# Attention, mixing, weight rounding and the first MLP tile placed by a plan in time

## The chip, the cores and the metric

The kernel runs on one core of a Trainium2 chip. The core has five engines that run side by side: TensorE (PE in the profile, its weight loads PEld), VectorE (DVE), ScalarE (ACT), GpSimd (POOL) and SyncE (SP, which here only issues DMAs). Each engine takes its instructions strictly in the order in which the program lists them for it; semaphores make it wait for other engines or for DMAs. The metric is the device time of one execution in microseconds (us); lower is better.

## The reference

Two parts follow each other. The first is causal attention with a decaying bias over 8 batches, 8 heads, 576 positions and head size 64:

```python
scores = scale * np.matmul(q, k.transpose(0, 1, 3, 2))
cum = np.cumsum(np.maximum(s, 0.0), axis=-1)
bias = -(cum[:, :, :, None] - cum[:, :, None, :])
scores = np.where(causal, -1000000000.0, scores + np.minimum(bias, 0.0))
attn = softmax(scores)          # with + 1e-09 in the denominator
x = np.matmul(attn, v)          # then [8, 576, 512]
```

The second mixes by a two-dimensional Fourier transform, normalises, and runs an MLP of width 2048:

```python
mixed = np.real(np.fft.fft(np.fft.fft(x, axis=1), axis=2))
u = x + mixed
un = (u - mean(u)) / np.sqrt(var(u) + 1e-06)
out = u + np.maximum(un @ w_ch1, 0.0) @ w_ch2
```

All of it is single precision. The kernel keeps that precision on TensorE by splitting numbers into a high and a low part ("h" and "l" in the names) and adding three products, high by high, high by low and low by high. The MLP weights arrive as 64-bit floating-point words and are rounded to 32 bits on the chip.

## The kernel before

**Attention.** Work goes by pairs of heads, `i` from 0 to 31, four pairs to a batch. For each pair `load` fetches q and k, `high` (L613, L615, ACT) and `low` (L630 DVE, L633 POOL, with two DMAs that move rows between partitions) split them, `maxes` (L654 PE, L661 DVE) computes the rows' maxima from high-part scores, and a small transpose and DMA (L666 to L669) put them into the operand as one more row. `scores` (L686, L687 PE) then computes transposed scores with the maximum already taken off, ACT takes the exponential into `P` (L690), and POOL zeroes the upper triangle (L693, L696). `av` (L718) multiplies by V, `recip` (L733 to L739) inverts the row sums and spreads them over partitions by a round trip through memory, and `finish` (L754 to L758) scales. While pair `i` has its scores taken, pair `i-1` is in `av`, pair `i+1` in `maxes` and `low`, pair `i+2` in `high`.

**Mixing.** Once a batch's four pairs are finished, `folds` (L448 to L464) adds and subtracts mirrored positions and `fourier` (L481 to L538) does the two transforms as matrix products, adds them to x and stores the sum in `uD`.

**Weights.** There are 16 chunks `f`, each in four pieces of 256 columns. `rounded` (L78 to L89) loads one piece and rounds it with four DVE instructions, one on ACT and one on POOL. `convert_w` does so for the first `NC = 6` chunks during attention, with one buffer, and stores the result in `wD`; `load_w` fetches those again, rounds the other ten itself, splits each into high and low (L115 ACT, L117 DVE or POOL) and keeps the second layer's part in `w2D`. The chunks live in three pools that take over memory as attention (`N0 = 3` chunks, then up to `N1 = 8`) and the last mixing give theirs back.

**MLP.** Tokens go in nine tiles of 512. `ln_tile` normalises a tile, `plain` or `block` splits it. `first_tile` (L339 first product, L343 and L344 rectifier and split, L262 to L264 second product) runs chunk after chunk as weights become ready. The other eight tiles run in `fast_tile` (L378), a seven-product scheme that needs sums of weights (`sums_w`, L143 to L163) and of token blocks (`combine`).

**What sets the order.** In attention and the first tile the order comes from `weave`: each function is a generator that yields a cost of its own scale, and of several such streams the one least advanced in proportion to its total goes next. Only PE keeps that order exactly (`tc.manual_schedule(engines={PE})`); on the other engines the framework's own scheduler may reorder. From the second tile on all engines keep the written order (`tc.manual_schedule()`). The line that decides this for attention:

```python
order.enter_context(tc.manual_schedule(engines={mybir.EngineType.PE}))
```

Of the kernel before, what the change touches and what calls it, by code (L numbers as in the profile page):

```python
# [27 lines left out]
NC = 6  # L28
NC1 = 4.5
N0 = 3  # L30
# [4 lines left out]
CH = [(128, 0, 576, 0), (128, 128, 448, 128), (128, 256, 320, 256), (128, 320, 256, 384), (64, 320, 256, 512)]  # L35
# [5 lines left out]
def fused_kernel(ctx, tc, qkT, vA, sP, wP, tabD, tabS, corr, out):  # L41
# [31 lines left out]

    def rounded(pool, f, x, bufs):

        m = pool.tile([128, WC], I32, tag="wm", name="wm", bufs=bufs)
        raw = pool.tile([128, 2 * WC], I32, tag="raw", name="raw", bufs=bufs)
        nc.sync.dma_start(out=raw, in_=wP[f, :, WC * x:WC * x + WC].bitcast(I32))  # L78
        hi = raw.rearrange("p (n w) -> p n w", w=2)[:, :, 1]
        lo = raw.bitcast(U16).rearrange("p (n w) -> p n w", w=4)[:, :, 1]  # L80
        yield 0.0
        e = pool.tile([128, WC], I32, tag="we", name="we", bufs=bufs)
        nc.vector.tensor_scalar(e, hi, 0x7FF00000, None, op0=ALU.bitwise_and)  # L83
        nc.scalar.activation(e, e, AF.Relu, bias=wbias, scale=8.0)
        nc.vector.tensor_scalar(m, hi, 0xFFFFF, 0x100000, op0=ALU.bitwise_and, op1=ALU.bitwise_or)  # L85
        yield 0.4
        nc.vector.scalar_tensor_tensor(out=e, in0=hi, scalar=-0x80000000, in1=e, op0=ALU.bitwise_and, op1=ALU.bitwise_or)  # L87
        nc.vector.scalar_tensor_tensor(out=m.bitcast(F32), in0=lo, scalar=2.0 ** -16, in1=m, op0=ALU.mult, op1=ALU.add)  # L88
        nc.gpsimd.tensor_mul(e.bitcast(F32), m.bitcast(F32), e.bitcast(F32))  # L89
        yield 0.4  # L90
        return e.bitcast(F32)

    def convert_w(pool, lo, hi, bufs):

        for f in range(lo, hi):
            for x in range(1024 // WC):
                m = yield from rounded(pool, f, x, bufs)
                nc.sync.dma_start(out=wD[f, :, WC * x:WC * x + WC], in_=m)
                yield 0.2

    def load_w(pool, f):

        wh = pool.tile([128, 512], F32R, tag=f"wh{f}", name=f"wh{f}")
        wl = pool.tile([128, 512], F32R, tag=f"wl{f}", name=f"wl{f}")
        vh, vl = second()
        W[f], W2[f] = (wh, wl), (vh, vl)
        if f < NC:
            nc.sync.dma_start(out=wl.bitcast(F32), in_=wD[f, :, 0:512])
            nc.sync.dma_start(out=vl.bitcast(F32), in_=wD[f, :, 512:1024])
        n = 512 if f < NC else WC  # L110
        for x in range(1024 // n):
            h, low = (wh, wl) if x * n < 512 else (vh, vl)
            xs = slice(n * x % 512, n * x % 512 + n)
            m = low[:, xs].bitcast(F32) if f < NC else (yield from rounded(stage, f, x, nstage))
            nc.scalar.copy(h[:, xs], m)  # L115
            yield 0.2 * n / 512
            last_subs[x * n >= 512] = (nc.vector if x * n < 512 else nc.gpsimd).tensor_sub(low[:, xs], m, h[:, xs].bitcast(F32))  # L117
            yield 0.2 * n / 512
        nc.sync.dma_start(out=w2D[0, f], in_=vh.bitcast(F32))
        nc.sync.dma_start(out=w2D[1, f], in_=vl.bitcast(F32))  # L120

    last_subs = [None, None]
# [202 lines left out]
    def first_tile(t0):  # L325
        _, r = LN[t0]
        acc = accs()
        fetch, done = writer(t0, acc, r)
        bl = BL.pop(t0)
        for f in range(NF):  # L330
            while min(f + 2, NF) not in W and next(feed, None) is not None:
                pass
            wh, wl = W[f]
            h = bank("h")
            for k in range(2):
                i = 0
                for a, b in ((wh, 0), (wl, 0), (wh, 1)):
                    for j in range(4):
                        nc.tensor.matmul(h[:, 256 * k:256 * k + 256], a[:, j * 128:(j + 1) * 128], bl[j // 2, k][b][:, j % 2], start=i == 0, stop=i == 11)  # L339
                        i += 1  # L340
            zh = zp.tile([128, TOK], F32R, tag="zh", name="zh", bufs=3)
            zl = zp.tile([128, TOK], F32R, tag="zl", name="zl", bufs=3)
            nc.scalar.activation(zh, h, AF.Relu)  # L343
            nc.vector.scalar_tensor_tensor(out=zl, in0=h, scalar=0.0, in1=zh.bitcast(F32), op0=ALU.max, op1=ALU.subtract)  # L344
            for g in groups():
                g()
            held.append((acc, zh, zl, f, done))
            yield 1.0
        for _ in range(3):
            fetch()  # L350

# [67 lines left out]
    cor = fft.tile([33, 258], F32R, name="cor")  # L419
    eh = fft.tile([33, 289], F32R, name="eh")  # L420
    nc.vector.memset(eh.bitcast(F32), 0.0)
# [5 lines left out]
    nc.vector.memset(Aw[:, 576:577], 0.0)  # L427

    def load_tables():
        for i in range(2):  # L430
            nc.gpsimd.dma_start(out=dcos[i], in_=tabD[i, :, :, 0:258])
            nc.gpsimd.dma_start(out=dsin[i], in_=tabD[i, :, :, 258:514])
            nc.gpsimd.dma_start(out=scos[i], in_=tabS[i, 0:97, 0])
            nc.gpsimd.dma_start(out=ssin[i], in_=tabS[i, 0:96, 1])
# [4 lines left out]
    FOURIER = 8900  # L439

    def folds(b, xa, xs):
# [3 lines left out]
        e = fft.tile([1, 289], F32, tag="e", name="e")  # L445
        for jj in range(2):
            a = Aw
            nc.vector.tensor_add(a[:, 0:576], xa[:, jj], xs[:, jj])  # L448
            bb = fft.tile([128, 576], F32, tag="Bw", name="Bw")
            nc.gpsimd.tensor_sub(bb, xa[:, jj], xs[:, jj])  # L450
            yield 1.0
            d = fft.tile([128, 289], F32, tag="Df", name="Df")
            nc.vector.tensor_add(d, a[:, 0:289], a[:, 576:287:-1])
            split(De[0][:, jj], De[1][:, jj], d)
            yield 1.0
            d = fft.tile([128, 289], F32, tag="Df", name="Df")
            nc.vector.tensor_sub(d[:, 0:288], bb[:, 1:289], bb[:, 575:287:-1])
            split(Do[0][:, jj], Do[1][:, jj], d[:, 0:288])
            yield 1.0
# [5 lines left out]
        folded[b] = (De, Do)  # L465

    folded = {}
    FOLDS = 7
    MIX = ((0.3, 0.25), (0.3, 0.4), (1, 0.35), (1, 0.05))

    def fourier(b, xa, xs):
# [402 lines left out]
    for _ in feed:  # L874
        pass
# [178 lines left out]
```

## Time and profile before

| | |
|---|---|
| median of 3 runs | 1455.16 us (1451.71 to 1459.55) |
| the profiled execution | 1451.0 us, span 1449.3 us, mean TensorE clock 0.959 |
| busy, share of the span | PE 1307.2 us (90%), DVE 891.4 (62%), ACT 640.7 (44%), POOL 513.7 (35%) |
| attention, to the last product with V | from 0 to 565 us |
| rest of mixing, first tile, second tile | 565 to 842 us |
| tiles 3 to 9 | 842 us to the end |

The shares over the span are a mean over stages that differ, so a table of stretches is the view to begin with. A clock below 1 in a stretch is the share of full speed that TensorE was granted there. A wait is put down to the instruction that came last among those it waited for. A busy PE is not always PE at its peak, since the ends of its matmuls are modelled.

### The profile page before, as it was taken

The numbers are of one execution on the slowest core, as the hardware profiler recorded it, in microseconds if no ns is written. First come the engines' busy times: TensorE is split into PE (matmuls) and PEld (weight loads), VectorE is DVE, ScalarE is ACT, GpSimd is POOL, SyncE is SP. The second block draws the span as 40 slices with busy tenths as digits, with TensorE's granted clock in tenths as the row PEclk, the third lists the DMA queues.
The fourth block names the chain that finished last, engine by engine and source line by source line (L and its number), as shares of the span: only waits on it lengthen the run. The fifth ranks groups of instructions, "written<-read, shape, count | busy, mean of one in ns | idle before, by whom it ended". The sixth has DMA issues, their size and how long they took to land.

```text
span 1449.3 us, 21855 instructions
## 1 busy us (share of the span) xinstructions
PE 1307.2 (90%) x7534; PEld 1111.8 (77%) x7534; DVE 891.4 (62%) x2018; ACT 640.7 (44%) x1507; POOL 513.7 (35%) x526
## 2 busy tenths in 40 slices
PE   4898979898989897697759999999999999999998
PEld 3675867676867675686548888888888888888887
DVE  6667687778677777577987754445445444554423
ACT  4675756566656656243433333333333333323321
POOL 6345465655546566464465211110211102021100
PEclk9998989999989998799979999999999999999999
DMA  8565556556555555534543353443435244342433
GB/s 205 138 175 143 155 143 180 144 161 177 149 156 141 168 130 184 181 103 164 162 136 118 103 187 102 145 133 127 164 102 180 98 145 146 124 167 88 146 116 116
DMA packets 125657, 210.18 MB, mean 145 GB/s; under 512 B 16488, under 2 KB 41417, under 8 KB 125547
## 3 DMA queue, kind: packets, MB, share of 16 engines
q1 hardware_dynamic: 123099, 204.79, 46.7%
q0 software_dynamic: 1632, 2.43, 0.8%
q10 hardware_dynamic: 816, 1.57, 0.3%
q8 instruction: 59, 0.97, 0.3%
q14 instruction: 51, 0.42, 0.1%
HBM read 153.33 MB, written 31.46 MB: 127 GB/s over the span
## 4 chain that ended last, share of the span: by engine, by line
PE 45%; DVE 8%; POOL 4%; DMA 2%; issue 1%; ACT 1%; SPq 0%; POOLq 0%; DVEq 0%; ACTq 0%
PE b L378 21%; PE acc L263 8%; PE acc L264 8%; PE acc L262 8%; POOL we L89 1%; DVE we L87 1%; DVE wm L85 1%; DVE we L83 1%; DVE bl L231 1%; POOL w2l L117 1%; DVE wm L88 1%; POOL t L210 0%; DMA rd<-sums 0%; DVE wl L117 0%; DMA rb<-rd 0%
## 5 line engine op out<-in xcount | busy, mean ns | idle before, releaser
L264 PE MATMUL acc<-zl,w2h 128*128 128x512 f32 x576 | 230.2, 401 | 11.1 <-DVE zl L344 11.1
L262 PE MATMUL acc<-zh,w2h 128*128 128x512 f32 x576 | 230.7, 401 | 7.2 <-ACT zh L343 7.2
L263 PE MATMUL acc<-zh,w2l 128*128 128x512 f32 x576 | 229.8, 399 | 0.0
L718 PE MATMUL pavB<-P,va 128*128 128x320 f32 (+2 forms) x640 | 198.3, 399 | 7.7 <-ACT stage L722 7.1
L690 ACT ACTIVATE P<-ps 128x320 f32<-128x320 f32 (+4 forms) x384 | 145.0, 390 | 112.1 <-PE ps L687 107.3
L654 PE MATMUL pm<-KQ 128*128 128x256 f32 (+4 forms) x384 | 157.0, 427 | 35.6 <-DVE Mx L661 18.7
L309 POOL TENSOR_TENSOR w<-w,o 128x512 f32<-128x512 f32 x32 | 43.7, 1375 | 382.5 <-DVE o L305 339.7
L686 PE MATMUL ps<-KQ 128*128 128x256 f32 (+3 forms) x384 | 153.1, 401 | 23.7 <-ACT P L690 12.9
L661 DVE CUSTOM_DVE_ANT_0 trash<-pm,amask 128x128 bf16<-128x128 f32 (+3 forms) x256 | 123.7, 483 | 74.1 <-PE pm L654 57.1
L370 ACT ACTIVATE zh<-cs 128x256 fp32r<-128x256 f32 (+1 forms) x128 | 67.2, 525 | 163.6 <-DVE cs L390 101.2
L264 PEld LDWEIGHTS acc<-zl,w2h 128*128 128x128 f32 x576 | 109.9, 191 | 37.8 <-DVE zl L344 12.4
L718 PEld LDWEIGHTS pavB<-P,va 128*128 128x128 f32 (+1 forms) x640 | 105.0, 194 | 30.9 <-issue 12.6
L371 DVE SCALAR_TENSOR_TENSOR zl<-cs,zh 128x256 fp32r<-128x256 f32 (+1 forms) x128 | 75.7, 592 | 79.3 <-ACT zh L370 79.3
L262 PEld LDWEIGHTS acc<-zh,w2h 128*128 128x128 f32 x576 | 110.1, 191 | 14.6 <-ACT zh L343 9.0
L687 PE MATMUL ps<-q,k 128*128 128x256 f32 (+3 forms) x384 | 120.2, 316 | 0.6 <-POOL q L633 0.6
L378 PEld LDWEIGHTS b<-bh,wh 128*128 128x128 f32 x512 | 96.3, 189 | 28.4 <-DVE cs L390 6.2
L654 PEld LDWEIGHTS pm<-KQ 128*128 128x128 f32 (+1 forms) x384 | 70.4, 186 | 61.6 <-DVE Mx L661 27.2
L633 POOL TENSOR_TENSOR q<-qk,q 64x576 fp32r<-64x576 f32 x64 | 99.9, 1575 | 42.7 <-DMA q<-KQ 36.4
L263 PEld LDWEIGHTS acc<-zh,w2l 128*128 128x128 f32 x576 | 110.2, 191 | 5.0
L686 PEld LDWEIGHTS ps<-KQ 128*128 128x128 f32 (+1 forms) x384 | 72.6, 189 | 49.8 <-ACT P L690 19.1
L378 PE MATMUL b<-bh,wh 128*128 128x256 f32 x512 | 102.9, 282 | 4.9 <-DVE cs L390 4.9
L378 PE MATMUL b<-bh,wl 128*128 128x256 f32 x512 | 103.4, 284 | 0.0
(173 smaller groups left out, 2859.7 us busy)
## 6 DMA issues: line engine op xcount, KB each, us to landing
w2h<-w2D SPq DMA_DIRECT2D x128, 256.0 KB
w2l<-w2D SPq DMA_DIRECT2D x128, 256.0 KB
qk<-in_qkT_dram SPq DMA_DIRECT2D x32, 576.0 KB
raw<-in_wP_dram SPq DMA_DIRECT2D x64, 256.0 KB
va<-in_vA_dram SPq DMA_DIRECT2D x32, 480.0 KB
q<-KQ SPq DMA_DIRECT2D x32, 288.0 KB
k<-KQ SPq DMA_DIRECT2D x32, 288.0 KB
rb<-rd SPq DMA_DIRECT2D x64, 144.0 KB
```

What stands on the lines that cost most here:

```text
L262: nc.tensor.matmul(acc[j], a[:, cs], y, start=f == 0, stop=False)
L263: nc.tensor.matmul(acc[j], b[:, cs], y, start=False, stop=False)
L264: nc.tensor.matmul(acc[j], a[:, cs], z, start=False, stop=f == NF - 1)
L371: nc.vector.scalar_tensor_tensor(out=y[1][:, at], in0=src, scalar=0.0, in1=y[0][:, at].bitcast(F32), op0=ALU.max, op1=ALU.subtract)
L378: nc.tensor.matmul(p[:, 0:256], a[:, j * 128:(j + 1) * 128], b[:, j], start=start and i == 0, stop=i == 5, skip_group_check=not start)
L633: nc.gpsimd.tensor_sub(q1[64:128, h], qk[0:64, h], q1[0:64, h].bitcast(F32))
L654: nc.tensor.matmul(p[:nq, :n], qy[:, h, 128 * c:128 * c + nq], ky[:, h, k0:k0 + n], start=True, stop=True)
L661: nc.vector.tensor_tensor_reduce(out=trash[:nq, :n], in0=p[:nq, :n], in1=amask[:nq, m0:m0 + n], scale=1.0, scalar=first if x else NEG, op0 ...
L686: nc.tensor.matmul(p[:nk, :n], ky[:, h, ksl], qy[:, h, a:a + n], start=True, stop=False)
L687: nc.tensor.matmul(p[:nk, :n], k1[:, h, ksl], q1[:, h, a:a + n], start=False, stop=True)
L690: nc.scalar.activation(P[:nk, o:o + a + n - lo], p[:nk, lo - a:n], AF.Exp, scale=0.125)
L718: nc.tensor.matmul(p[:, a - lo:n], va[:nk, c, vs], P[:nk, o:o + w], start=c == 0, stop=c == cs[-1])
```

## The change

One planner takes the place of `weave` for everything from the first pair to the end of the first tile, and all five engines keep the order it gives. The functions are still generators, but each step now names the engine, a cost in microseconds, what it depends on (events) and the buffer it takes from a ring; DMA issues on SP are steps too. `Flow.run` repeatedly takes the step that can start first, by the planned times of its dependencies, its engine and its ring, and among those within 0.05 us on the same engine the one with the earliest due time. It runs while the program is written; nothing of it runs on the chip.

With it go these edits: 12 chunks instead of 6 are rounded during attention, in two streams with two buffers; 2 chunks instead of 3 are loaded ahead of the end of attention; the five PSUM banks that maxima and V products shared become three and two; the last key block of each head, which had 64 rows or columns, is widened to 128 with fixed zeros; the first tile opens when the last pair is finished; normalisation and token blocks of the second tile (`prepare`) and the first two sums of weights (`sums_flow`) are steps of the plan. `fast_tile` stays as it is.

```diff
-NC = 6
-NC1 = 4.5
-N0 = 3
+NC = 12
+NV = 2
+N0 = 2
...
-CH = [(128, 0, 576, 0), (128, 128, 448, 128), (128, 256, 320, 256), (128, 320, 256, 384), (64, 320, 256, 512)]
+CH = [(128, 0, 576, 0), (128, 128, 448, 128), (128, 256, 320, 256), (128, 320, 256, 384), (128, 320, 256, 512)]
...
+    order = ctx.enter_context(ExitStack())
+    order.enter_context(tc.manual_schedule())
...
+    T = 16.0
...
+        eq.memset(KQ[i][0:64, 1].bitcast(F32), 0.0)
+        eq.memset(KQ[i][64:128, 1, :, S:640].bitcast(F32), 0.0)
+        eq.memset(KQ[i][0:2, 1, :, 0:S].bitcast(F32), 1.0)
+        ek.memset(KQ[i][0:64, 0].bitcast(F32), -1.0)
+        ek.memset(KQ[i][64:128, 0, :, S:640].bitcast(F32), 0.0)
+        eq.memset(K1[i][:, :, S:640].bitcast(F32), 0.0)
...
+            e = yield dve(576, ev("k", i, h))
+            nc.vector.tensor_sub(k1[0:64, h, 0:S], qk[64:128, h], ky[64:128, h, 0:S].bitcast(F32))
...
+                e, hold = yield pe(mm(n), ev("rows", i), ev("k", i, h), ev("q", i, h), ring=(ring("psm", 3), 1))
+                p = psm.tile([128, 512], F32, tag="m", name="pm", bufs=3)
+                nc.tensor.matmul(p[:, :n], qy[:, h, 128 * c:128 * c + 128], ky[:, h, k0:k0 + n], start=True, stop=True)
...
+                    e, phold = yield pe(cost, *deps, ring=(ring("psv", 2), 2 if h else 1))
+                    p = psm.tile([128, 512], F32, tag="v", name="pav", bufs=2)
...
+    def pair(i):
+        yield from load(i) if i >= 3 else ()
+        flow.add(high(i), T * (i - 1.6), 0.7)
+        yield wait(ev("q", i, 1))
+        flow.add(low(i), T * (i - 1.2), 1.0)
+        flow.add(maxes(i), T * (i - 1) + 14.0)
+        yield wait(ev("row", i), ev("low", i), *(at(("scored", i - 1)) if i else ()))
+        flow.add(scores(i), T * i - 1.0)
+        yield wait(ev("va", i), ev("P4", i, 0))
+        flow.add(av(i), T * i + 7.0)
+        yield wait(ev("sums", i))
+        flow.add(recip(i), T * (i + 1) + 8.0)
+        yield wait(ev("rb", i), *(at(("out", i - 1)) if i else ()))
+        flow.add(finish(i), T * (i + 1) + 16.0)
...
+    def conversion(part):
+        for k in range(part, 4 * NC, NV):
+            f, x = divmod(k, 4)
...
+            yield from piece("attb", f, x, WC, NV, store)
...
+    T0 = T * NP + 10.0
...
+    def first_tile(t0):
+        yield wait(ev("plain"), ev("open"))
...
+    def tail():
+        yield wait(ev("scored", NP - 2), ev("low", NP - 1), ev("row", NP - 1), ev("q", NP - 1, 1))
+        atop_ctx.close()
...
+        flow.add(plain(tiles[0]), T * (NP - 1), 0.5)
...
+        for f in range(N0):
+            yield from load_w("attb", f, NV, w0)
+        yield wait(ev("out", NP - 1), *(ev("wD", f) for f in range(NC)), *at(*((n, f) for n in ("W", "W2") for f in range(N0))))
+        attb_ctx.close()
...
+        ev("accp").t = ev("open").t = ev("out", NP - 1).t
         for f in range(N0, N1):
+            yield from load_w("stage1", f, 4, w1)
+        yield wait(ev("u", NB - 1), *at(*((n, f) for n in ("W", "W2") for f in range(N0, N1))))
         stage_ctx.close()
         fft_ctx.close()
...
+        flow.add(prepare(tiles[1]), T0 + 60.0, 1.0)
         for f in range(N1, NF):
+            yield from load_w("stage2", f, 3, wB)
...
+        ev("late").t = ev("W", NF - 1).t
+        flow.add(sums_flow(), T0 + 80.0)
...
+    for part in range(NV):
+        flow.add(conversion(part), T * 1.5, T * (NP - 3) / (NC * 4 * 8) * NV)
+    flow.add(tail(), 0.0)
+    flow.add(first_tile(tiles[0]), T0, 2.8)
+    flow.run(ev("first"), ev("prepared"), ev("sums_w"))
...
+class Flow:
+    LAG = {"PE": 0.35, "ACT": 0.2, "DVE": 0.2, "POOL": 0.25}
...
+    def run(self, *goals):
+        while any(g.t is None for g in goals):
+            ready = [(t, s) for s in self.live for t in (self.start(s[3]),) if t is not None]
+            t, s = min(ready, key=lambda x: (x[1][3][0] is not None, x[0]))
+            engine = s[3][0]
+            t, s = min(((u, v) for u, v in ready if v[3][0] == engine and u <= t + 0.05), key=lambda x: x[1][1])
+            self.place(s, t)
...
+        if engine == "SP":
+            self.free[engine] = t + 0.6
+            self.wire = max(self.wire, t) + cost / 190.0
+            e = Event(self.wire + 2.2)
...
+def dve(n, *deps, ring=None):
+    return "DVE", 0.1 + n * 0.0011, deps, ring
...
+def mm(n):
+    return 0.012 + n / 2300
```

More of the change, by code (lines that the diff above doesn't have):

```diff
@@ L93, in convert_w @@
[L93 to L120, printed above, removed]
@@ L323, in writer @@
         return fetch, done
[L325 to L350, printed above, removed]
     def fast_tile(t0, side):
@@ new lines, in fused_kernel, with cum_rows @@
+    nc.vector.memset(Aw[:, 576:577], 0.0)
+    flow.free.update(DVE=9.0, ACT=8.5, POOL=14.0, PE=2.0)
+    def cum_rows():
+        for w in range(2):
+            yield dma(100)
+            nc.sync.dma_start(out=cumD[w, 0], in_=cumhl[:R, w * S:(w + 1) * S].bitcast(F32))
+            yield dma(100)
+            nc.sync.dma_start(out=cumD[w, 1], in_=fixed.bitcast(F32))
+        yield dma(100)
+        nc.sync.dma_start(out=cumD[2, 0], in_=minus)
+        e = yield dma(100)
+        nc.sync.dma_start(out=cumD[2, 1], in_=zero)
+        ev("cumD").t = e.t
@@ new lines, in block_flow @@
+    def block_flow(t0, k, src, done, *deps):
+        e, hold = yield ("ACT", 0.65, deps, (ring("blocks", 9), 1))
+        h = bp.tile([128, 2, 256], F32R, tag="bh", name="bh", bufs=9)
+        low = bp.tile([128, 2, 256], F32R, tag="bl", name="bl", bufs=9)
+        nc.scalar.copy(h, src)
+        BL.setdefault(t0, {})[k] = (h, low)
+        e = yield dve(512, e)
+        nc.vector.tensor_sub(low, src, h.bitcast(F32))
+        done.add(e)
+        if isinstance(k, tuple):
+            ev("block", k).hold = hold
@@ L915, in fused_kernel, with __init__, add, next @@
     order.close()
-def take(gen, quota):
-    done = 0.0
-    while done < quota:
+class Event:
+    def __init__(self, t=None):
+        self.t = t
+        self.hold = None
+class Last:
+    def __init__(self, event, n):
+        self.event, self.n, self.t = event, n, 0.0
+    def add(self, e):
+        self.t = max(self.t, e.t)
+        self.n -= 1
+        if not self.n:
+            self.event.t = self.t
+class Ring:
+    def __init__(self, n):
+        self.held = [Event(0.0) for _ in range(n)]
+        self.k = 0
+    def next(self):
+        return self.held[self.k % len(self.held)]
+    def take(self, readers):
+        e = Event()
+        self.held[self.k % len(self.held)] = e
+        self.k += 1
+        return Last(e, readers)
@@ L932, in chain @@
         yield from g
-def idle(cost):
-    yield cost
-def later(gen, n):
-    for _ in range(n):
-        yield 1.0
-    yield from gen
-def weave(*streams):
-    for _ in mixed(*streams):
-        pass
-def mixed(*streams):
-    live = [[g, total, 0.0] for g, total in streams if g is not None]
-    while live:
-        s = min(live, key=lambda s: s[2] / s[1])
-        try:
-            s[2] += next(s[0])
-        except StopIteration:
-            live.remove(s)
-        else:
-            yield 1.0
 def _tables():
```

1080 lines of the change are left out of this document (700 added, 380 removed).

## The prediction

> **What bounds the kernel now.** The profiled execution took 1451.0 us, with a span of 1449.3 us, so 1.7 us lie outside the span; the median of the three runs is 1455.16 us, 0.3% above. All sums below are made against 1451.0.
>
> I read the table of stretches first, since the kernel has stages with different limits. Columns: length, busy us (and instructions) of PE, PEld, DVE, ACT, POOL, then the granted TensorE clock, the DMA share and GB/s.
>
> ```profile
> 30.00:130.00 100.00, 86.14 (x423) 66.89 (x422) 64.01 (x182) 66.95 (x162) 47.18 (x52) 0.95 0.63 160
> 130.00:560.00 430.00, 383.68 (x2079) 307.79 (x2080) 314.46 (x880) 265.64 (x665) 239.28 (x253) 0.95 0.56 155
> ...
> 565.00:587.00 22.00, 15.86 (x68) 13.77 (x69) 14.94 (x30) 10.71 (x22) 10.73 (x10) 0.61 0.63 208
> 587.00:616.00 29.00, 17.79 (x100) 15.42 (x100) 15.48 (x28) 7.04 (x14) 11.23 (x11) 0.76 0.49 161
> 616.00:737.00 121.00, 99.70 (x568) 83.02 (x567) 99.66 (x217) 49.31 (x110) 61.94 (x72) 0.94 0.46 147
> 737.00:763.00 26.00, 10.34 (x42) 8.18 (x41) 22.02 (x33) 8.67 (x18) 16.00 (x16) 0.69 0.33 111
> 763.00:842.00 79.00, 76.10 (x468) 67.10 (x467) 57.27 (x94) 30.31 (x67) 28.33 (x27) 0.99 0.38 120
> 842.00:927.00 85.00, 85.00 (x533) 76.34 (x532) 40.83 (x72) 27.55 (x64) 11.84 (x9) 1.00 0.42 137
> ```
>
> From 842 us to the end PE never pauses; that is MLP tiles 2 to 8, and the edit leaves their code alone. So 1449.3 - 842 = 607 us stand as they are. Before 565 us is attention (32 head pairs, the last attention-times-V product ends at 565): PE is busy 86 to 89% and DVE 73% (314.46 of 430), so no engine is full and it is the order that costs. Between 565 and 842 lies what I call the change-over: rest of the mixing, first MLP tile, second tile. It lasts 277 us, and in 616:737 DVE is busy 82% while PE, at a clock of 0.94, waits. In 737:763 PE works 10 of 26 us.
>
> The chain of waits shows what DVE and the DMAs do there (start us, length, what):
>
> ```profile
> 594.01 2.68 DMA rd<-sums
> ...
> 597.25 2.93 DMA rb<-rd
> 600.30 0.77 DVE xr L754
> ...
> 604.37 0.76 DVE Aw L448
> ...
> 651.93 2.93 DMA uD<-xa
> 655.33 4.43 DMA raw<-in_wP_dram
> ...
> 842.38 0.71 PE b L378 x6
> ```
>
> The last pair is finished at 600 us, 35 us after its last product; its batch is folded, mixed and stored by 655; only then is memory free for the weight chunks 8 to 15, which are loaded raw and rounded by DVE until about 737, ten us a chunk.
>
> **The change part by part.**
>
> *Conversion taken out of the change-over.* Of 16 weight chunks, 4 pieces each, 6 were rounded during attention, now 12: 24 pieces move. One piece is four DVE instructions, one on ACT, one on POOL and, where it is done early, a raw load and a store. DVE's groups in 616:737 (what, count | busy, mean ns of one):
>
> ```profile
> L87 DVE SCALAR_TENSOR_TENSOR we<-raw,we 128x256 int32<-128x256 int32 x40 | 22.7, 567 | 1.4 <-ACT we L84 1.0
> L85 DVE TENSOR_SCALAR wm<-raw 128x256 int32<-128x256 int32 x39 | 19.8, 508 | 0.0
> L83 DVE TENSOR_SCALAR we<-raw 128x256 int32<-128x256 int32 x39 | 19.1, 491 | 6.4 <-DMA raw<-in_wP_dram 6.4
> L88 DVE SCALAR_TENSOR_TENSOR wm<-raw,wm 128x256 f32<-128x256 uint16 x40 | 18.1, 452 | 0.6
> ```
>
> 567 + 508 + 491 + 452 = 2.02 us a piece; 24 pieces are 48.4 us of DVE less. In the five stretches DVE is busy 14.9 + 15.5 + 99.7 + 22.0 + 57.3 = 209 us; 161 stay. What can this give at most? PE's own need. A fast tile streams 7 x 8 x 6 products of 256 columns and 192 of 512, 184,320 columns with 528 matmuls; the last row has 533 in 85.0 us, so 84.2 us a tile, 0.457 us per 1000 columns. The first tile has 16 x 24 of 256 and 192 of 512: 196,608 columns, 89.8 us. The last batch's mixing has 23,000 columns (10.5 us), and of the batch before it some 17,000 are left at 565 (7.8 us). With two normalisation sums (2 us by the same rate) and the second tile PE needs 89.8 + 84.2 + 10.5 + 7.8 + 2 = 194 us of the 277; at most 83 us can go, and nothing need go if another chain holds the end.
>
> I charge three rests against the 83. First, the first tile now opens only when the last pair is finished. The chain above from the sums to the product takes 594.01 to 601.07, 7 us; with the copies and the sums' own DMA ahead of it I estimate 13 us after the last product, of which the mixing left over covers 7.8: 5 us of idle PE. Second, the later chunks: the fold-mix-store chain of the last batch lasts 604 to 655, 51 us, and is not shorter by code. From an opening 13 us after the last product, memory is free at 64 us, four chunks instead of eight are rounded at ten us each, so the last weights stand at about 104 us; PE reaches them after 5 + 7.8 + 10.5 + 89.8 x 15/16 = 107 us. That hides, narrowly; but the sums of weights for the second tile are traced after the last chunk, and the 26 us stretch 737:763 shows what they cost where nothing covers them. The normalisation and block copies that share it are now moved ahead; I leave 8 us. Third, the second tile still computes these sums on the way, and runs slower than a later one: 5 us, from 79 us for 468 matmuls against 85 for 533 (79 - 468 x 85/533 = 4.4). Sum 18; the change-over gains 65 us, with bounds 0 and 83.
>
> A sign of what stalls cost beside their length is the timeline around the longest one (start, length, what, idle before it):
>
> ```profile
> 607.78 0.79 PE L264 MATMUL acc<-zl,w2h 128*128 128x512 f32 x1 [10.85 <-DVE zl L344]
> ...
> 608.80 0.63 PE L264 MATMUL acc<-zl,w2h 128*128 128x512 f32 x1
> ...
> 614.88 0.39 PE L262 MATMUL acc<-zh,w2h 128*128 128x512 f32 x1
> ```
>
> After 10.85 us of idleness a matmul takes 0.63 instead of 0.39 us for some 6 us, so a long stall costs about 3 us more than itself. By the Trainium skill, "TensorE: Matmul & The Clock Gate", section "What's actually happening", the array falls to half its clock after an idle window of about 3.4 us and is back after some 3.4 us of steady work; the trace agrees on the half rate and shows nearly twice that time until it is back. By the skill's figure the three stretches with clocks under 0.8 would hold less to regain; the sum above does not use it.
>
> *The same pieces put into attention.* Here they cost less each, by the groups of 60:560:
>
> ```profile
> L89 POOL TENSOR_TENSOR we<-wm,we 128x256 f32<-128x256 f32 x20 | 15.0, 748 | 36.1 <-DVE we L87 15.0 <-issue 9.7 <-DVE wm L88 9.0
> ...
> L84 ACT ACTIVATE we<-we,wbias 128x256 int32<-128x256 int32 x20 | 10.2, 508 | 8.3 <-DVE we L83 8.2
> ...
> L83 DVE TENSOR_SCALAR we<-raw 128x256 int32<-128x256 int32 x20 | 9.9, 496 | 1.1 <-DMA raw<-in_wP_dram 1.0
> L88 DVE SCALAR_TENSOR_TENSOR wm<-raw,wm 128x256 f32<-128x256 uint16 x20 | 8.4, 422 | 0.5
> L87 DVE SCALAR_TENSOR_TENSOR we<-raw,we 128x256 int32<-128x256 int32 x20 | 8.4, 421 | 0.2
> ...
> L85 DVE TENSOR_SCALAR wm<-raw 128x256 int32<-128x256 int32 x20 | 6.9, 347 | 0.0
> ```
>
> 496 + 422 + 421 + 347 = 1.69 us, times 24 = 40 us of DVE, 12 of ACT, 18 of POOL. DVE had 430 - 314 = 116 us idle in 130:560, so the 40 fit: it goes from 73 to some 82%. Bounds: nothing, or 40 us if DVE's idle time sits where it cannot be used. SP gets 48 more issues. In the timeline of one pair such an issue lasts
>
> ```profile
> 448.72 1.43 SPq L98 DMA_DIRECT2D wD<-we  x1
> ...
> 450.26 0.37 SPq L78 DMA_DIRECT2D raw<-in_wP_dram  x1
> ```
>
> so 24 x (1.43 + 0.37) = 43 us at most over some 530 us on SP's queue; behind them queue the pair's own loads and row moves. I cost this at nothing, hidden by DMAs issued a pair ahead, and 9.4 MB more at 0.56 share move the wires little; if that cover goes it is inside the 40. The read-back of chunks 6 to 11 takes the place of raw loads of the same size.
>
> *The new order of attention.* What can it gain? In 30:560 PE is idle 13.9 + 46.3 = 60 us, and the waits that it names in 130:560 are (engine, what, for whom: total us, times, longest)
>
> ```profile
> PE pm L654 <- DVE Mx L661: 15.4, 7, 5.3
> PE ps L686 <- ACT P L690: 11.7, 10, 2.1
> PE pavB L718 <- ACT stage L722: 5.5, 9, 1.2
> ```
>
> all order and buffers, none a full engine. A plan that put each instruction right could take nearly 60 us; one that is off gains nothing, or loses (the last rival). I take half of each bound: half of the 60 gained, half of the 40 lost, 30 - 20 = 10 us gained.
>
> *Small edits.* Fixed rows are set on wider tiles and three short memsets are added per buffer. The start shows
>
> ```profile
> L579 POOL MEMSET KQ<- 2x1152 f32 x3 | 3.1, 1047 | 0.0
> ...
> L587 POOL MEMSET amask<- 128x640 bf16 x1 | 0.6, 621 | 0.0
> ```
>
> For the first buffer the wider set adds 128/1152 of 1.05 us twice on POOL, and two short ones at most 0.62 each: 0.2 to 1.5 us before the first product; I take 1. The blocks made full (128 rows or columns where there were 64) stream the same free size: nothing.
>
> **Sum.** 1451.0 - 65 - 10 + 1 = 1377 us.
>
> **The rivals.**
>
> *The plan keeps its own pace.* Its pairs are due every 16 us; before, 25 pairs took the 430 us of 130:560, 17.2 each. Then attention loses 25 x 1.2 = 30 us, all the conversion being hidden, and the change-over 75: 1451 - 105 + 1 = 1347, down to 1309 at both bounds (83 + 60). For: no engine above 90%. Against: DVE at 16 us a pair would be at 314.46/25 + 1.69 x 24/32 = 13.8 us of 16, with strict order on every engine.
>
> *The change-over stays a chain.* The out-fold-mix-store chain holds memory as before and only the four chunks fewer after 655 count: 4 x 10 = 40 us, less 15 for stalls that come out behind it, and attention gains nothing: 1451 - 25 = 1426. For: 594 to 655 is DMA and small steps. Against: PE has six chunks to work on meanwhile.
>
> *The moved work is paid in full in attention.* DVE's subtraction for the low half of k and its fold sum show (count, duration ns min/median/max)
>
> ```profile
> L630 DVE TENSOR_TENSOR k<-qk,KQ x64: 748/1040/2952, 7.7 to 507.2; 64x576 fp32r<-64x576 f32 x64
> ```
> ```profile
> L448 DVE TENSOR_TENSOR Aw<-xa,xs x16: 737/745/1876, 119.5 to 608.0; 128x576 f32<-128x576 f32 x16
> ```
>
> so the same instruction takes up to 2.2 us more at times. If each moved POOL product (748 ns) also holds up DVE for its length, a piece costs 1.69 + 0.75 = 2.44 us, 58 us for 24; with no gain in order the time is 1451 - 65 + 58 = 1444; with 40 alone, 1426. I put this case at 1435. Beside it stands the Trainium skill, "SBUF — State Buffer": DVE instructions with two SBUF inputs and GpSimd share a port pair which one holds for a whole instruction while the other is blocked. The spread of the two rows agrees with such a lock; no row shows who held what.
>
> *The order holds PE up (slower).* Place: the score maxima of pairs 8 to 31. Their PSUM ring shrinks from 5 banks shared with the V products to 3 of their own (and 2 for those). The plan prices the low-half subtraction at 0.1 + 576 x 0.0011 = 0.73 us where the row above has a median of 1.04, and the maxima hang behind it on DVE. The two engines already wait on each other, PE 15.4 us as quoted and, in 60:560,
>
> ```profile
> DVE trash L661 <- PE pm L654: 51.0, 33, 7.2
> ```
>
> With PE in strict order a late DVE stops PE, the exponentials and then DVE. It decides once a pair takes 65/25 = 2.6 us longer, 19.8 us; at 21 us it costs 25 x 3.8 = 95 us: 1451 - 65 + 95 = 1481. Against: PE's order was fixed before too, and DVE's 73% leaves slack.
>
> **How the numbers follow.** Forecast 0.42, plan's pace 0.18, chain 0.10, paid in attention 0.13, slower order 0.15; 0.02 are left for no visible change. The likeliest case alone spans 1347 to 1407 (attention between 10 us lost and 30 gained, change-over 55 to 75 gained). The range reaches down into the second case and up through the chain and paid cases to the edge of the slower one: 1320 to 1455. Within 0.5% of 1455 (1448 to 1462; the three runs lie 0.5% apart, so less than this can't be told from no change) falls the upper edge of the paid case and the 0.02: 0.05. Slower 0.17 is the last rival and a little of its neighbours; faster 0.78.
>
> **What would show it.** The steps are right if the last exponential comes at 535 to 560 us, the first product of the first tile some 13 us after the last V product, DVE's groups of the rounding show 16 pieces after that instead of 40, the first to second tile takes about 110 us, and tile 2 starts near 767 with 607 us behind it. Wrong: a pair period of 19 us or more with PE waiting for the maxima; a PE gap of over 20 us ahead of the first tile or ahead of the second; or a change in the last 607 us.

## The result, and the profile after

The changed kernel takes 1537.35 us (median of 4 runs, 1534.19 to 1542.16) where the kernel before, run beside it, takes 1455.68 us. The ratio is 1.056, with a 95% interval of 1.052 to 1.061: slower by 82 us, where the sum of the prediction forecast 74 us of gain. The profiled execution took 1536.2 us, with a span of 1534.5 us and a mean TensorE clock of 0.929 (0.959 before).

The difference between the two profiled executions is 85 us, and four moments in the traces place it:

| | before | after | difference |
|---|---|---|---|
| first exponential (ACT, `P`) | 30.0 | 43.3 | +13 |
| from there to the end of the last V product | 535 | 634 | +99 |
| from there to the start of the third tile (the change-over) | 277 | 250 | -27 |
| from there to the end | 607 | 607 | 0 |

So attention holds all of the loss. The table of stretches of the changed kernel (length, busy us and instructions of PE, PEld, DVE, ACT, POOL, then the granted TensorE clock, DMA share, GB/s):

```profile
43.00:130.00 87.00, 67.68 (x327) 56.25 (x327) 51.86 (x152) 47.74 (x119) 33.39 (x40) 0.89 0.47 126
130.00:665.00 535.00, 418.52 (x2185) 357.63 (x2185) 377.23 (x1027) 288.03 (x724) 264.93 (x285) 0.87 0.52 147
665.00:677.00 12.00, 11.34 (x69) 9.97 (x69) 5.97 (x17) 8.16 (x22) 4.14 (x7) 1.00 0.42 142
677.00:690.00 13.00, 4.49 (x24) 3.24 (x22) 5.16 (x8) 7.04 (x13) 10.94 (x10) 0.78 0.41 139
690.00:725.00 35.00, 29.98 (x173) 27.07 (x174) 23.01 (x34) 12.05 (x26) 11.79 (x9) 0.84 0.47 163
725.00:775.00 50.00, 50.00 (x331) 45.66 (x330) 19.33 (x35) 15.63 (x29) 19.10 (x18) 1.00 0.55 187
775.00:826.00 51.00, 34.01 (x150) 29.09 (x149) 42.74 (x88) 21.53 (x46) 22.07 (x27) 0.77 0.34 114
826.00:848.00 22.00, 10.84 (x61) 9.43 (x60) 13.86 (x25) 5.64 (x12) 12.33 (x15) 0.77 0.40 143
848.00:927.00 79.00, 76.43 (x466) 67.77 (x465) 56.93 (x94) 30.68 (x69) 28.00 (x27) 0.98 0.37 120
```

In 130:665 PE is idle 535 - 418.5 = 116 us; before, 46 us of 430. No engine is fuller for it: DVE is busy 71% (73% before). An engine that has more to do would show a higher share; here all shares fall together, which is what a wait in a strict order looks like. The waits that PE names over the whole span (engine, what it waited for: total us, times, longest):

```profile
PE ps L569 <- DMA KQ<-mt: 113.6, 29, 21.0
PE pm L519 <- DVE Mx L529: 21.3, 14, 7.0
PE h L1145 <- ACT wh L983: 13.8, 7, 3.0
```

One wait holds 113.6 us: the first score of a pair (L569, L686 before) waits for the small DMA that lays the maxima into the operand as a row. Of these, 21.0 us are the first pair's, ahead of the first exponential; the other 28 waits make 92.6 us. The same waits in the kernel before, over its whole span:

```profile
PE pm L654 <- DVE Mx L661: 18.7, 13, 5.3
...
PE ps L686 <- DMA KQ<-mt: 6.7, 7, 2.1
```

The timeline of the changed kernel around one such place (start, length, engine, what; in brackets idle time before it and what ended it):

```profile
309.72 0.28 PE L541 MATMUL pmt<-ident,Mx 128*10 128x128 f32 x1 [1.12 <-DVE Mx L529]
...
311.14 0.25 ACT L545 CAST mt<-pmt 10x128 fp32r<-10x128 f32 x1
311.32 0.34 SPq L664 DMA_DIRECT2D rd<-sums  x1
311.76 0.82 SPq L548 DMA_DIRECT2D KQ<-mt  x1
...
315.00 0.55 PE L569 MATMUL ps<-KQ 128*128 128x256 f32 x1 [5.00 <-DMA KQ<-mt]
```

PE transposes the maxima at 309.72 and has nothing listed between that and the scores that need them, so it stands for 5.00 us while ACT copies, SP issues another DMA first, and the row lands. PE can't go round the scores: its order is fixed. The scores stand too early in PE's list.

### The profile page after: what moved, and what is told of

Read it like the earlier page. It is cut to its first block, busy times and chain, and to the rows that moved or that the text cites. A ratio compares the mean times of both kernels' runs of the same rounds, so it can differ in the third digit from the quotient of the medians.

```text
span 1534.5 us, 21929 instructions
## 1 busy us (share of the span) xinstructions
PE 1313.6 (86%) x7534; PEld 1150.8 (75%) x7534; DVE 885.6 (58%) x2011; ACT 633.8 (41%) x1495; POOL 504.9 (33%) x528
## 4 chain that ended last, share of the span: by engine, by line
PE 67%; DVE 12%; DMA 9%; ACT 4%; SPq 3%; issue 3%; POOL 2%; DVEq 0%; POOLq 0%; ACTq 0%
PE b L301 20%; PE acc L212 8%; PE acc L213 8%; PE acc L214 8%; PE pav L629 8%; DMA KQ<-mt 6%; PE ps L569 4%; PE ps L570 3%; PE h L1145 3%; PE pm L519 2%; PE pz L794 2%; DMA xs<-xr 2%; DVE trash L529 1%; ACT P L575 1%; DVE Aw L732 1%
## 5 line engine op out<-in xcount | busy, mean ns | idle before, releaser
L569 PE MATMUL ps<-KQ 128*128 128x256 f32 (+2 forms) x384 | 145.9, 385 | 117.6 <-DMA KQ<-mt 113.6
L214 PE MATMUL acc<-zl,w2h 128*128 128x512 f32 x576 | 227.1, 394 | 0.0
L629 PE MATMUL pav<-P,va 128*128 128x320 f32 (+4 forms) x896 | 219.3, 388 | 1.2 <-ACT stage L641 0.6
L629 PEld LDWEIGHTS pav<-P,va 128*128 128x128 f32 x896 | 173.2, 209 | 38.5 <-issue 7.5
L575 ACT ACTIVATE P<-ps 128x320 f32<-128x320 f32 (+4 forms) x384 | 140.5, 392 | 144.6 <-PE ps L570 139.9
L569 PEld LDWEIGHTS ps<-KQ 128*128 128x128 f32 x384 | 85.8, 224 | 132.7 <-issue 61.8
L519 PE MATMUL pm<-KQ 128*128 128x256 f32 (+3 forms) x384 | 128.6, 384 | 40.9 <-DVE Mx L529 21.3
L570 PE MATMUL ps<-Q,K 128*128 128x256 f32 (+2 forms) x384 | 131.1, 345 | 0.0
L519 PEld LDWEIGHTS pm<-KQ 128*128 128x128 f32 x384 | 75.9, 211 | 59.6 <-DVE Mx L529 32.1
L487 POOL TENSOR_TENSOR Q<-qk,Q 64x576 fp32r<-64x576 f32 x64 | 98.4, 1549 | 32.7 <-DMA Q<-KQ 20.3
```

What stands on the lines that cost most here:

```text
L214: nc.tensor.matmul(acc[j], a[:, cs], z, start=False, stop=f == NF - 1)
L487: nc.gpsimd.tensor_sub(q1[64:128, h], qk[0:64, h], q1[0:64, h].bitcast(F32))
L519: nc.tensor.matmul(p[:, :n], qy[:, h, 128 * c:128 * c + 128], ky[:, h, k0:k0 + n], start=True, stop=True)
L569: nc.tensor.matmul(p[:, :n], ky[:, h, ksl], qy[:, h, a:a + n], start=True, stop=False)
L570: nc.tensor.matmul(p[:, :n], k1[:, h, ksl], q1[:, h, a:a + n], start=False, stop=True)
L575: nc.scalar.activation(P[:, o:o + a + n - lo], p[:, lo - a:n], AF.Exp, scale=0.125)
```

## The experiments

All kernels: the median, the ratio to the kernel before measured beside each and its 95% interval. The last three columns are the moments of the table above (us), read from the profiled execution, whose time lies up to 8 us from the median (row_dep: 1484.7).

| kernel | us | ratio | first exponential | last V product ends | third tile starts |
|---|---|---|---|---|---|
| before | 1455 | | 30.0 | 565 | 842 |
| changed | 1537.4 | 1.056 [1.052, 1.061] | 43.3 | 677 | 927 |
| row_dep | 1492.4 | 1.027 [1.024, 1.030] | 39.0 | 630 | 876 |
| waits_kept | 1444.6 | 0.996 [0.994, 0.998] | 44.0 | 587 | 835 |
| ring5 | 1569.4 | 1.077 [1.073, 1.082] | 40.4 | 707 | 958 |
| pe_only | 1494.0 | 1.026 [1.022, 1.031] | 43.7 | 651 | 886 |
| nc6 | 1565.7 | 1.079 [1.077, 1.080] | 40.4 | 674 | 958 |
| waits_nc6 | 1473.5 | 1.012 [1.009, 1.015] | 41.3 | 582 | 867 |
| old_nc12 | 1492.3 | 1.029 [1.027, 1.031] | 29.5 | 647 | 887 |
| all16 | 1445.5 | 0.994 [0.991, 0.996] | 34.3 | 621 | 836 |
| start12 | 1461.4 | 1.004 [1.002, 1.006] | 34.0 | 601 | 849 |
| start14 | 1442.6 | 0.991 [0.987, 0.994] | 33.1 | 600 | 832 |
| start16 | 1435.7 | 0.986 [0.983, 0.990] | 34.1 | 606 | 826 |
| start16_pe | 1500.8 | 1.031 [1.025, 1.037] | 29.0 | 666 | 890 |

**Why do the scores stand too early?** The code answers with a suspicion. `scores` begins with `_, hold = yield wait(ev("row", i), ev("low", i), ...)`. A `wait` names no engine, and `Flow.run` delivers such steps at once, as soon as their dependencies have a planned time, even one that lies ahead. `place` hands back an event with that time, but the caller drops it: the next step, `pe(2 * mm(n), ring=...)`, names no dependency at all. So the plan knows when the row lands and forgets it, and stands the scores on PE as soon as PE is free. The plan runs while the program is written, so its own times can be written out: there the first score of a pair starts on average 5.0 us ahead of the planned landing of its row (31 of 32 pairs early, up to 11.4 us).

**The row named again at the scores alone (row_dep).**

```diff
-                e, hold = yield pe(2 * mm(n), ring=(ring("ps", 3), 1))
+                e, hold = yield pe(2 * mm(n), ev("row", i), ev("low", i), ring=(ring("ps", 3), 1))
```

> One dependency is added in the plan: each score product names the row of maxima and the low halves as what it needs, so that the plan can no longer put it ahead of their landing. The instructions are the same, their order is new. Theory A (the planner forgets the time of a wait that has no engine, so the scores stand on PE some 5 us before their row lands): PE's waits of the scores for the row's DMA fall from 114 us to under 40, the last exponential moves from 672 to 585 to 610 us, the time from 1537 to 1450 to 1480 us. Theory B (the 24 pieces moved into attention and the PSUM ring of three set the pace, and the wait for the row is only where it shows): the waits go over to the maxima and DVE, and the time stays above 1515 us.

Measured: 1492.4 us, 45 us less than the changed kernel, between what the two theories gave. PE's waits of this kernel:

```profile
PE pm L519 <- DVE Mx L529: 65.2, 44, 14.0
...
PE ps L569 <- DMA KQ<-mt: 8.4, 4, 7.4
```

The named wait is gone (113.6 to 8.4 us), but 44 us of it come back as waits for DVE's maxima. Other steps drop their waits too, the fold sums (`Aw`, L732) among them: in this kernel's plan the first sum of each batch stands 2.3 to 6.5 us ahead of its mirrored rows. DVE waits there, and in places a maximum stands right behind it on DVE. DVE's own waits of this kernel in 30:600:

```profile
DVE Aw L732 <- DMA xs<-xr: 15.7, 6, 5.7
```

That these 15.7 us make a part of PE's 65.2 is an inference; no run mends the folds alone. The next one mends all dropped waits together.

**Every dropped wait kept (waits_kept).** A step may now never start ahead of what its own stream has waited for.

```diff
+        self.now = 0.0
...
-        self.send([gen, due, step, None], None)
+        self.send([gen, due, step, None, self.now], None)
...
-            ready = [(t, s) for s in self.live for t in (self.start(s[3]),) if t is not None]
+            ready = [(max(t, s[4]), s) for s in self.live for t in (self.start(s[3]),) if t is not None]
...
         else:
             e = Event(t)
+            s[4] = max(s[4], t)
+        self.now = s[4]
```

> The planner itself is mended: a wait without an engine keeps its time, and the steps behind it in the same function, and the functions it starts, are not planned earlier. This covers the scores, the folds that wait for the mirrored rows, and the first tile. Theory A: as with the one dependency, and besides DVE's and POOL's waits for the mirrored rows (25 and 30 us) fall by half; time 1440 to 1475 us. Theory B: above 1515 us.

Measured: 1444.6 us, 93 us less than the changed kernel and 0.4% less than the kernel before (interval 0.2 to 0.6%). Its waits and stretches:

```profile
PE pm L519 <- DVE Mx L529: 33.1, 38, 5.2
PE ps L569 <- DMA KQ<-mt: 19.2, 6, 14.2
```
```profile
130.00:575.00 445.00, 390.36 (x2136) 328.32 (x2134) 348.41 (x995) 277.97 (x703) 252.79 (x275) 0.94 0.62 173
...
686.00:733.00 47.00, 31.53 (x152) 26.41 (x151) 38.36 (x81) 19.66 (x44) 21.93 (x25) 0.82 0.35 104
733.00:755.00 22.00, 9.05 (x52) 7.82 (x51) 14.19 (x24) 5.44 (x12) 12.84 (x16) 0.77 0.53 179
```

PE is busy 88% of 130:575 again, at a clock of 0.94 instead of 0.87. Of the 19.2 us of row waits 14.2 are the first pair's, at the start. Every engine does the work that it does in the changed kernel, and the change-over is the same (248 against 250 us); only the order in attention differs, and it is worth 90 us (677 to 587). This settles the main cause. The plan's own end of its last scores bears it out: 517 us in the changed kernel, where the chip's last exponential comes at 672; 585 against 625 in row_dep; 567 against 581 here, and 12 of these 14 us lie ahead of the first score. It also shows that an honest plan is no faster here than the old order: from pair 5 to pair 30 (starts of the transposes `pmt` on the chip, of the first scores in the plan) a pair takes 17.5 us in its own times and 17.4 on the chip, where the kernel before takes 17.1.

**Maxima and V products share five banks again (ring5).** The edit sets the changed kernel's two rings, three banks and two, back to one of five.

```diff
-ring=(ring("psm", 3), 1)
+ring=(ring("psm", 5), 1)
...
-ring=(ring("psv", 2), 2 if h else 1)
+ring=(ring("psm", 5), 2 if h else 1)
```

> The changed kernel with the five PSUM banks shared again by the maxima and the V products, in the plan's rings too; waits are still dropped by the planner. Theory A (dropped waits): the scores still stand ahead of their rows, so PE's waits for the row's DMA stay above 90 us and the time between 1500 and 1545 us. Theory C, the slower rival of the prediction (the ring of three holds PE up at the maxima): attention loses 60 us or more, time below 1475 us.

Measured: 1569.4 us, 32 us more than the changed kernel and more than either theory gave. PE's waits:

```profile
PE ps L569 <- DMA KQ<-mt: 121.1, 30, 19.0
...
PE pav L629 <- DVE Mx L529: 16.3, 5, 8.9
```

The prediction's slower rival put the loss on the smaller ring of the maxima. With the five banks back the row's wait is longer still, and V products now wait for maxima as well. The rival's place is refuted. Why five shared banks make a plan that is too early slower still, no run here tells apart.

**Only PE keeps the plan's order (pe_only).** As in the kernel before, the framework reorders the other engines.

```diff
-    order.enter_context(tc.manual_schedule())
+    order.enter_context(tc.manual_schedule(engines={mybir.EngineType.PE}))
...
+    order.close()
+    order.enter_context(tc.manual_schedule())
```

> The changed kernel with only PE keeping the plan's order up to the end of the first tile; the framework's scheduler may reorder the other engines, as before the change. Theory A: PE's order is what is wrong, so its waits for the row's DMA stay above 80 us and the time stays above 1500 us. Theory D (strict order on ACT, DVE, POOL and SP's queue is what costs): SP's queue no longer holds the rows back and the time falls below 1475 us.

Measured: 1494.0 us. The row's wait is halved, not gone:

```profile
PE ps L569 <- DMA KQ<-mt: 54.2, 23, 7.6
```

The time falls between what the two theories gave. So the strict order on the other engines had a part in it. One place shows in the traces: from the end of the row's copy on ACT to the issue of its DMA, 1.4 us pass in the mean instead of 2.1 in the changed kernel (0.3 before). That is a cure for the symptom; start16_pe below asks the same question of a plan that keeps its waits.

**What the moved conversion costs and gives (nc6, waits_nc6, old_nc12).** Six chunks early instead of twelve in the changed kernel (`NC = 6`), the same on top of waits_kept, and twelve early in the kernel before with its old order:

```diff
-NC = 6
-NC1 = 4.5
+NC = 12
+NC1 = 10.5
```

> The changed kernel with 6 chunks rounded during attention instead of 12, everything else as changed. Theory A: attention hardly moves (last exponential 672 to between 655 and 675), since its pace comes from the misplaced scores, and the change-over gets longer by some 30 to 50 us: 1560 to 1590 us. Theory B: attention loses 40 to 60 us and the time stays within 1500 to 1540 us.

> The planner that keeps the time of its waits, with 6 chunks rounded during attention instead of 12. Beside the same planner with 12 it gives the price of the moved pieces in an order that holds. If they lie in DVE's idle time, as the prediction took half of them to, the last exponential moves from 581 to not below 570 and the change-over gets 30 to 50 us longer: 1465 to 1490 us. If they are paid in full, attention loses 40 us or more and the time stays at 1435 to 1450 us.

> The kernel before, with 12 chunks rounded during attention instead of 6, and its spreading of the pieces over the pairs scaled to that; the order is otherwise woven as before. It tells what the moved pieces do without the plan. Theory A (the plan's order alone is what costs): the change-over loses 30 to 65 us and attention gains at most 40, time 1395 to 1440 us. Theory B (the moved pieces set the pace of attention): attention gains 60 us or more, time 1455 us or above.

Measured: nc6 1565.7 us. Its attention ends at 674, 3 us ahead of the changed kernel's, and its change-over is 284 us instead of 250. On the kept waits the same pair gives 582 against 587, and 285 against 248. So under the plan the 24 pieces cost 3 to 5 us of attention, nearly 3 of them ahead of the first exponential, and give 34 to 37 us of change-over. PE's waits in the first tile say what they give; of nc6 and of waits_nc6:

```profile
PE h L1145 <- ACT wh L983: 32.8, 16, 5.1
```
```profile
PE h L1145 <- ACT wh L983: 32.5, 15, 7.2
```

First products wait 13.8 us for weights in the changed kernel, 32.8 and 32.5 us without the moved pieces. The first branch of both expectations held. In nc6 PE's row waits are 75.5 us behind the first pair, instead of 92.6 in the changed kernel, and from the first exponential on attention is as long (633 and 634 us); so the total of one wait is not by itself the time that mending it gives.

In the old order the same move is dear. old_nc12 takes 1492.3 us: its change-over falls from 277 to 240 us, but attention ends at 647 instead of 565. The expectation that put all the loss on the dropped waits missed here; the one that called the moved work dear held. PE's waits and the stretch:

```profile
PE pm L654 <- DVE Mx L661: 55.8, 30, 4.6
```
```profile
130.00:640.00 510.00, 419.91 (x2107) 330.56 (x2106) 356.94 (x979) 282.67 (x702) 265.63 (x280) 0.89 0.54 149
```

DVE is busy 70% of the stretch and does 42 us more work in it than in the 430 us before (357 against 314; 40 by the prediction's groups), so its work alone does not make 82 us. PE's waits for maxima grew by 37 us, and its granted clock was 0.89 instead of 0.95. DVE also waits for raw loads, which go into the single conversion buffer; in 130:600:

```profile
DVE we L83 <- DMA raw<-in_wP_dram: 19.6, 7, 4.4
```

In the kernel before these waits are below 1.3 us there. Whether this buffer, the weave's proportions or the framework's order on DVE makes the maxima late was not varied.

**All sixteen chunks early (all16), and a quiet start (start12, start14, start16).** all16 is waits_kept with 16 chunks, the five shared banks, the preparation of the second tile due 30 us earlier, and bulk stores and raw loads held back until the first pair's row has landed:

```diff
-NC = 12
+NC = 16
...
+        yield wait(ev("row", 0))
...
-        flow.add(prepare(tiles[1]), T0 + 60.0, 1.0)
+        flow.add(prepare(tiles[1]), T0 + 30.0, 1.0)
```

The start kernels go back to three banks and two, and give each number of early chunks a due spacing that leaves room for it: 12 chunks at `T = 17.0`, 14 at 17.5, 16 at 18.0 (16.0 in the change).

> The planner that keeps its waits, with all 16 chunks rounded during attention, so that none is left for the change-over; besides the five PSUM banks are shared again, the stores of the bias rows and the first roundings come after the first row of maxima, and the second tile's normalisation is due 30 us earlier. If the second layer's ring of four buffers together with the rounding of chunks 12 to 15 (11 us a chunk on the chip) holds up the end of the first tile, the products of those chunks now follow each other at 6 us, the change-over falls from 248 to 215 to 230 us and the time to 1405 to 1430 us. If PE or the sums for the second tile hold it up instead, it stays above 240 us and the time at 1440 us or above.

> The planner that keeps its waits, 12 chunks, PSUM banks three and two as in the change; the stores of the bias rows and the first roundings come after the first row of maxima, pairs are due every 17 us, the second tile's normalisation 30 us earlier. If the late first score (44 us here against 30 before) is the queue of stores and raw loads ahead of the first pair's own moves, it comes at 30 to 36 us and the time falls by about as much, to 1425 to 1438 us; if not, the first score stays above 40 us and the time at 1440 to 1450 us.

> As the one with 12 chunks and the later stores, with 14 chunks rounded during attention and pairs due every 17.5 us. Two chunks less in the change-over take 10 to 20 us from it, by 11 us a chunk where their rounding holds PE up; eight more pieces cost attention 0 to 14 us (1.69 us of DVE each). Time 1415 to 1435 us.

> All 16 chunks rounded during attention, with the PSUM banks three and two; pairs due every 18 us. Beside the kernel that had five shared banks it tells whether the shared banks or the 16 more pieces made attention there 34 us longer than with 12 chunks. If the banks: last V product at 585 to 600 us, time 1410 to 1430 us. If the pieces: last V product at 610 us or later, time 1435 to 1450 us.

Measured: all16 takes 1445.5 us. The half of its expectation on the change-over held (215.5 us, the shortest of all), the half on the total missed, because attention now ends at 621. PE's waits say where:

```profile
PE ps L570 <- ACT P L576: 28.1, 25, 6.5
PE pav L630 <- DVE Mx L530: 25.5, 14, 7.7
```

V products wait for maxima again, as in ring5, which shares the banks too, and scores wait for exponentials.

start12's first exponential comes at 34.0 instead of 44.0 us, as expected of the start; but its last V product comes at 601 instead of 587, and the total is 1461.4 us, 17 more than waits_kept. That missed. The spacing of 17 us changed with the start, so which of the two costs attention these 24 us (10 earlier at its start, 14 later at its end) is not settled. The loss is spread over the pairs (18.6 us each from pair 5 to pair 30, against 17.4), and the plan does not show it: its last scores end at 564 us, the chip's last exponential comes at 596.

start14 takes 1442.6 us: its change-over is 232 us, 16 less than start12's, and its attention no longer, as expected of the chunks, but from the slower start12 the time misses 1415 to 1435. start16's last V product at 606 falls between the two branches of its expectation, its time at the foot of the second; since the due spacing differs from all16's too, it does not part the banks from the pieces. It takes 1435.7 us: **1.4% less than the kernel before (interval 1.0 to 1.7%), and the best of all kernels here**. Stretches and waits of start16:

```profile
130.00:600.00 470.00, 405.26 (x2143) 336.41 (x2144) 372.63 (x1063) 284.36 (x724) 266.36 (x293) 0.91 0.62 174
616.00:728.00 112.00, 105.46 (x655) 95.06 (x656) 62.20 (x90) 38.27 (x74) 44.08 (x39) 0.94 0.54 181
728.00:746.00 18.00, 9.98 (x53) 8.46 (x52) 12.51 (x22) 6.05 (x12) 8.42 (x10) 0.81 0.36 123
```
```profile
PE pm L520 <- DVE Mx L530: 42.9, 51, 5.7
```

start16 pays 41 us in attention (606 against 565) and takes 57 us back in the change-over (220 against 277), where PE is busy 94% of the first tile.

**Is strict order on all engines good or bad, once the plan is honest (start16_pe)?** start16 with only PE in the plan's order, by the edit of pe_only.

> As the kernel with 16 chunks and a planner that keeps its waits, but only PE keeps the plan's order up to the end of the first tile, the framework's scheduler may reorder the rest. Theory A (with the waits kept, the plan's order is a good one on all engines): the time rises from 1436 us, to 1445 us or above. Theory D (strict order on ACT, DVE, POOL and SP costs even so, as it did by 43 us with the waits dropped): it falls below 1430 us.

Measured: 1500.8 us, 65 more than start16. The sign has turned: on a plan that forgets waits, freedom for the other engines gains 43 us; on one that keeps them it loses 65. PE's waits in 30:730:

```profile
PE ps L570 <- ACT P L576: 39.1, 16, 9.3
PE pm L520 <- DVE Mx L530: 32.7, 37, 6.7
PE ps L570 <- DMA KQ<-mt: 22.5, 7, 6.9
```

From the row's copy to the issue of its DMA 4.0 us pass in the mean, 1.7 in start16.

## Why the prediction was wrong, point by point

**The new order of attention, with the moved pieces in it: 10 us gained forecast, 99 lost.** This is the step that failed. I bounded the plan's gain by PE's idle time (60 us), took half, and took the description of the planner at its word, that it places steps "by the planned times of its dependencies". For every dependency named through `wait` it doesn't, and with these times kept the kernel is 93 us faster (waits_kept). Even then attention takes 543 us from the first exponential to the last V product, 8 more than before: the gain that I forecast is not there either. The price was readable before the run: follow one pair's row from `pmt` to the first score in the code, and ask which event the score names. The slower rival had the right sign, and its decision point (a pair over 19.8 us) was passed, since pairs from 5 to 30 take 20.4 us. But its mechanism was another: the wait for the maxima grew only from 18.7 us before to 21.3, and the ring was not the cause (ring5).

**The moved pieces: half of 40 us forecast.** Under the plan they cost 3 to 5 us, near the lower bound; DVE's idle time could be used. In the old order they cost 82 us (old_nc12), outside both bounds that I gave, 40 and the rival's 58. A bound made of busy time does not bound a change of order.

**The change-over: 65 us forecast, 27 measured.** The sum was PE's need of 194 us and rests of 18, so 212; it took 250. By the stretches above PE is busy 4.5 + 30.0 + 50.0 + 34.0 + 10.8 + 76.4 = 206 us there, 12 more than its need, with a granted clock of 0.77 to 0.84 in four of the stretches, and idle 44 us instead of 18. The rests one by one:

- The first tile opens 13 us after the last V product (677 to 690), as forecast; PE is idle 8.5 of these, where I allowed 5, and 5 more in 690:725.
- The later chunks were to hide narrowly. They did not: 17 us of idleness in 775:826. Memory was free at 749, 72 us after the last product (64 forecast), but the rounding of the last four chunks (all instructions on tile `raw` in 690:830: count, ns min/median/max, first and last start) began later:

```profile
L933 SPq DMA_DIRECT2D raw<-in_wP_dram x16: 327/332/399, 763.8 to 814.9; - x16
L938 DVE TENSOR_SCALAR we<-raw x16: 227/286/818, 775.5 to 819.5; 128x256 int32<-128x256 int32 x16
```

The first raw load is issued at 763.8, 15 us after memory is free, and the first piece reaches DVE at 775.5, another 12 us later, after normalisation steps of the second tile that the plan stands ahead of it. The code has a gate that I had not read: `load_w` of chunk `f` waits for `ring("w2", 4)`, so the loads of chunk 12 come in the plan only after the second product of chunk 8, which runs at 761.9 to 764.8 on the chip. From there a chunk takes 11 us (ten forecast), with DVE busy 42.74 of 51 us. Which part of the 27 us each of these would give back alone was not tried; all16, which has no later chunks, has a change-over of 215.5 us, next to the 212 forecast.

- The sums of weights leave 11 us of PE's 22 in 826:848 idle (8 allowed); the second tile runs as forecast, 79 us.

That the 24 pieces are what shortens the change-over is right: without them it takes 284 us. The old order's 277 us with six early chunks was thus 7 us shorter than the plan's.

**The start: 1 us forecast, 13 measured.** I priced the memsets and not the queue. The chain of waits of the changed kernel (start, length, what):

```profile
16.68 12.03 DMA Q<-KQ
28.77 13.70 DMA KQ<-mt
42.52 0.58 PE ps L569
...
54.98 1.95 DMA KQ<-mt
```

The stretches around the two rows of the same kind (columns as above):

```profile
16.00:43.00 27.00, 4.44 (x10) 2.31 (x10) 6.63 (x20) 0.25 (x1) 8.00 (x8) 1.00 1.12 233
50.00:60.00 10.00, 8.59 (x47) 6.96 (x46) 7.28 (x23) 5.95 (x14) 5.17 (x6) 1.00 0.12 31
```

Two moves on the first pair's path land 12.0 and 13.7 us after issue, with stores of bias rows and raw loads of weights issued ahead of them; the DMA engines are full the whole time (a share of 1.12, counted by packets that overlap). A row of the same kind takes 1.95 us at 55 us, where they are at 0.12. With the bulk held back the first exponential comes at 34.0 us (start12; 34.3 in all16). By the Trainium skill, "DMA: Bandwidth & Descriptors", section "Anatomy of one DMA — SWDGE (gpsimd) path", the fixed part of a DMA issued by GpSimd is about 2.0 us. These rows are issued by SP, which that section does not treat; their 1.95 us lies beside the figure, their 13.70 us far above it.

**The end: 607 us forecast, 607 measured.** Tiles 3 to 9 did not move.

## What to carry to other kernels

When a kernel's order is made by its own planner, print for each step its planned start beside the planned landing of everything that it reads: a start ahead of a landing is a stall on every engine that keeps a strict order, as far as the plan's times hold, and needs no chip to be found. A plan's own end that is far from the chip's (517 against 672 us here) says in one number that something is missing, not what: start12 keeps its waits and is still 32 us apart. And busy time did not bound an edit that moves work into another order: the same 24 pieces cost 3 to 5 us in one order and 82 us in another.

## What the runs showed of the hardware

- A 5 KB row that reaches its place within 2 us when the DMA engines are at a share of 0.12 took 13.7 us while they were full (a share of 1.12). With the bulk held back the first exponential came 10 us earlier.
- Many short gaps went with a cost to TensorE beyond their length: with 28 row waits of 3.3 us in the mean, about one a pair, the granted clock in 130:665 was 0.87 (0.94 with the waits kept), and 2185 matmuls took 418.5 us, 0.192 us each, against 0.185 before and 0.183 with the waits kept. As far as the mix of matmuls is the same, that is an estimate of some 15 us over the stretch beside the idle time.
